# Decoding float64 weights in an attention and max-out kernel: a whole-word shift, a sign written by ScalarE, and a first-layer split in two instructions

## The chip, the cores and the metric

The kernel runs on one core of a Trainium2 chip. A core has a matrix engine (TensorE, PE in the profile, with its weight loads as PEld), VectorE (DVE), ScalarE (ACT), GpSimd (POOL) and a queue engine (SyncE, SP), which run their own instruction queues side by side and wait for each other by semaphores. The metric is the device time of one execution in microseconds; the time of a kernel is the median of its runs.

## The reference, cut to what matters

```python
# q, k, v: (8, 12, 448, 64)
q_n, k_n = rmsnorm(q, g_q), rmsnorm(k, g_k)      # over the last axis
scores = q_n @ k_n^T / sqrt(64)
attn = softmax(scores)
x = (attn @ v), heads side by side -> (3584, 768)
h = max(x @ w1, x @ w2, x @ w3)                  # w1, w2, w3: 768 x 768
out = (h @ w_out).astype(float32)                # w_out: 768 x 768
```

q, k, v and the gains come as float32. The four weight matrices come as float64, since they are scaled by a float64 number: each weight is two 32-bit words, and the kernel has to turn them into float32 and then into a pair of float16 parts.

## The kernel before, in words

**Attention.** The 96 heads are taken in pairs: 48 groups g, with the feed-forward part of a batch of six groups queued behind them. A group is 12 beats (`beat(g, i)`, i from 0 to 11), and for each of its four quarters c of the queries there are three beats. In the first, ScalarE makes the exponentials (`softmax`), TensorE multiplies the scores of the next quarter and, in the first six groups (g < PLAIN), transposes the exponentials of the quarter before (`turned`, two tiles per quarter); in the second, ScalarE copies those transpositions to SBUF (`pt`); in the third, VectorE takes the row maxima (`nm`) of the next scores. The first six groups work in float32 and turn their queries and keys on TensorE (`rows`, copied by ScalarE to `kt` and `qt`); the later groups work with pairs of float16 parts, and their weights are written as an upper part by ScalarE and a lower part by VectorE (`pp`). `thirds()` mixes the matmuls of the feed-forward part into the beats as it is queued.

**The order is written by hand.** Each engine runs its instructions in the order in which the program names them. `later(n, work)` puts a piece of work n beats on; work with `last=True` comes behind all other work of its beat. Nothing is reordered by a planner. Tiles of the PSUM pool `ps_m` (tag "m") have three buffers in turn, shared by `rows`, `turned`, `marks`, `most`, `spread` and `acc`: a new tile waits until the reader of the tile that had its buffer is done.

**Weights.** Blocks of 768 weights a partition are decoded one by one: 18 blocks of w1, w2, w3 at every fourth beat, then 6 blocks of w_out at every eighth (`BLOCK_BEATS`). A block is loaded into one of two `raw` buffers as pairs of words, low word first. In the profiled program `prep_block` does at its beat the rebias on ScalarE (the upper word, read as a float32, times 2^-112, in place), and two, three and four beats on the three stages of `decode` on VectorE: the top three bits of the low word are shifted down (from half-words), the sign is taken from the upper word into the low word's upper half, and one instruction shifts the upper word left by three and ORs the low word in. That gives the block as float32 in the place of its float16 parts. The next load into the buffer is issued one beat after the last stage (blocks of w_out: nine beats after the first).

**The first-layer split.** For every three blocks, `bound_in` measures a bound: 18 matmuls into `marks`, a maximum on VectorE (`most`, L172), a transposition (L157), a maximum over a row (`top`, L160), a matmul that spreads it (L164, again a tile named `most`), one VectorE instruction that reads it (L273), a root on GpSimd and three small instructions that make the scale `up`. Then each of the three blocks is split at steps of four beats: ScalarE scales it in place (L289) and casts it to float16 (L290), and two beats later GpSimd subtracts this from the scaled block (L293). The blocks of w_out are split in another way already: a scaled cast on ScalarE (L329) and one VectorE instruction (L334).

Of the kernel before, what the change touches and what calls it, by code (L numbers as in the profile page):

```python
# [8 lines left out]

F32 = mybir.dt.float32  # L10
U32 = mybir.dt.uint32
U16 = mybir.dt.uint16
BF16 = mybir.dt.bfloat16
F16 = mybir.dt.float16
AF = mybir.ActivationFunctionType
ALU = mybir.AluOpType
# [7 lines left out]
REBIAS = 2.0 ** -112  # L24
# [22 lines left out]
def qknorm_attention_maxout_ffn_kernel(  # L47
# [35 lines left out]
    nc = tc.nc  # L83
# [36 lines left out]
    def later(beats, work, last=False):  # L120

        due.setdefault(clock[0] + beats, ([], []))[last].append(work)
# [26 lines left out]
    def largest(column, done, gaps):  # L149


        top = sb.tile([1, 1], F32, name="top", bufs=2)
        box = []

        def turn():
            box.append(ps_m.tile([P, 512], F32, name="marks", tag="m"))
            nc.tensor.matmul(box[0][0:1, 0:P], column, ident, start=True, stop=True)  # L157

        def reduce():
            nc.vector.tensor_reduce(top, box[0][0:1, 0:P], axis=AX, op=ALU.max)  # L160

        def spread():
            box.append(ps_m.tile([P, 512], F32, name="most", tag="m"))
            nc.tensor.matmul(box[1][:, 0:1], ones, top, start=True, stop=True)  # L164

        at = 0
        for gap, work in zip(gaps, (turn, reduce, spread, lambda: done(box[1][:, 0:1]))):
            at += gap
            later(at, work)

    def row_largest(dst, src):
        nc.vector.tensor_reduce(dst, src, axis=AX, op=ALU.max, apply_absolute_value=True)  # L172
# [4 lines left out]
    w_sb = const.tile([P, NFT * NJ + 1, 2, NCT * P], F16, name="w_sb")  # L177
# [9 lines left out]
    def rebias(raw):  # L187


        upper = raw.bitcast(F32).rearrange("p (n t) -> p n t", t=2)[:, :, 1]  # L190
        nc.scalar.activation(upper, upper, AF.Copy, scale=REBIAS)

    def decode(raw, f, stage):

        words = raw.bitcast(U16).rearrange("p (n t) -> p n t", t=4)
        bits = raw.rearrange("p (n t) -> p n t", t=2)
        if stage == 0:
            nc.vector.tensor_scalar(
                out=words[:, :, 0], in0=words[:, :, 1], scalar1=13, scalar2=None,
                op0=ALU.logical_shift_right,  # L200
            )
        elif stage == 1:
            nc.vector.tensor_scalar(
                out=words[:, :, 1], in0=words[:, :, 3], scalar1=0x8000, scalar2=None,
                op0=ALU.bitwise_and,
            )
        else:
            nc.vector.scalar_tensor_tensor(
                out=f.bitcast(U32), in0=bits[:, :, 1], scalar=3, in1=bits[:, :, 0],
                op0=ALU.logical_shift_left, op1=ALU.bitwise_or,  # L210
            )
# [22 lines left out]
    def plain(t, n):  # L234
        return t[:, n + 1].rearrange("p a n -> p (a n)").bitcast(F32)

    def prep_block(n):
        kind, ft, j = blocks[n]
        raw = raws[n]
        f = plain(w_sb, n) if kind == "in" else plain(wo_sb, ft)  # L240
        rebias(raw)

        for stage in range(3):
            later(2 + stage, lambda stage=stage: decode(raw, f, stage), True)
        if kind == "out":
            later(5, lambda: row_largest(o_row[:, ft:ft + 1], f), True)
        later(5 if kind == "in" else 9, load_raw)
        if j == NJ - 1:
            later(5, lambda: bound_in(ft), True)
        elif kind == "out" and ft == NFT - 1:  # L250
            later(6, bound_out)

    def bound_in(ft):

        most = sb.tile([P, 1], F32, name="most", bufs=2)
        box = []

        def products():
            box.append(ps_m.tile([P, 512], F32, name="marks", tag="m"))
            for at in range(NJ * NCT):  # L260
                n, c = divmod(at, NCT)
                f = plain(w_sb, ft * NJ + n).bitcast(BF16)
                f = f.rearrange("p (n t) -> p n t", t=2)[:, c * P:(c + 1) * P, 1]
                nc.tensor.matmul(
                    box[0][:, 0:P], f, f, start=at == 0, stop=at == NJ * NCT - 1
                )

        def reduce():
            row_largest(most, box[0][:, 0:P])
            largest(most, clear, (2, 2, 3, 1))  # L270

        def clear(bound):
            nc.vector.tensor_scalar(  # L273
                out=most, in0=bound, scalar1=SQUARE, scalar2=LEAST ** 2,
                op0=ALU.mult, op1=ALU.max,
            )
            nc.gpsimd.tensor_tensor(out=w_up[:, ft:ft + 1], in0=most, in1=root, op=ALU.pow)
            later(2, scale)

        def scale():  # L280
            top, up = w_most[:, ft:ft + 1], w_up[:, ft:ft + 1]
            nc.vector.tensor_copy(top, up)
            nc.vector.reciprocal(up, top)
            nc.vector.tensor_scalar(
                out=up, in0=up, scalar1=2.0 * UP, scalar2=None, op0=ALU.mult
            )

            def upper(n, f):
                nc.scalar.activation(f, f, AF.Copy, scale=up)  # L289
                nc.scalar.copy(w_sb[:, n, 0], f)  # L290

            def lower(n, f):
                nc.gpsimd.tensor_tensor(  # L293
                    out=w_sb[:, n, 1], in0=f, in1=w_sb[:, n, 0], op=ALU.subtract
                )

            for j in range(NJ):
                n = ft * NJ + j
                f = plain(w_sb, n)
                later(2 + 4 * j, lambda n=n, f=f: upper(n, f), True)  # L300
                later(4 + 4 * j, lambda n=n, f=f: lower(n, f), True)

        later(2, products)
        later(4, reduce)
# [632 lines left out]
    for i, src in enumerate((g_q, g_k)):  # L937
        nc.scalar.dma_start(
            out=gains[:, i], in_=src.rearrange("(o d) -> o d", o=1).broadcast_to([P, D])
# [75 lines left out]
    def beat(g, i):  # L1015
# [102 lines left out]
        if decoded[0] < len(blocks) and clock[0] > due_at:  # L1118
            later(0, lambda n=decoded[0]: prep_block(n), True)
            decoded[0] += 1  # L1120
# [42 lines left out]
```

## Time and profile before

| What | Value |
|---|---|
| median of three runs | 1051.09 us (1048.96 to 1051.29) |
| the profiled execution | 1049.89 us, of which its span is 1047.7 us |
| TensorE, VectorE, ScalarE, GpSimd busy | 95%, 68%, 61%, 60% of the span |
| granted TensorE clock over the span | 0.99 |
| rebias (L191), first and last start | 19.5 and 217.4 us, 24 instructions |
| the split's cast (L290), first and last start | 68.5 and 190.4 us, 18 instructions |

The page counts for each engine how long its instructions ran; idle time is put down to what ended last before the engine went on. A group of instructions is a source line with its tiles: busy time, the mean of one, and the idle time just before them with its releaser. The timeline has the start and the duration of single instructions, with the idle time before them in brackets. Engines overlap, so busy time alone says nothing about the end; the work that a stage waits for does. The chain of waits that ended last is on TensorE from 430 us on.

### The profile page before, as it was taken

Reading aid. Unit: us, or ns where it says so; the run is one execution under the profiler, and the core shown is the slowest. Engines: PE = TensorE matmul, PEld = TensorE weight load, DVE = VectorE, ACT = ScalarE, POOL = GpSimd, SP = SyncE. Lnnn points to the kernel's source line nnn. Section 1 sums busy time; section 2 is a strip of 40 time slices with the busy share of each in tenths; the row PEclk is TensorE's granted clock in tenths of the full one; section 3 lists DMA queues with packets and bytes.
Section 4 is the critical chain, followed back from the end, with each engine's and each line's share of the span. In section 5 each row is a group of like instructions: output and inputs, shape, how many; then the busy total and the mean of one; then the engine's idle time right before and its main releaser. Section 6 shows DMA issues by size and latency. Waiting matters only on the chain.

```text
span 1047.7 us, 17338 instructions
## 1 busy us (share of the span) xinstructions
PE 991.5 (95%) x5958; PEld 530.3 (51%) x5958; DVE 707.5 (68%) x1322; ACT 638.6 (61%) x1437; POOL 625.9 (60%) x667
## 2 busy tenths in 40 slices
PE   4988879897899999999999999999999999999998
PEld 3554544343445555455555555555555555555555
DVE  4988889898667766677676857776677657661120
ACT  3778887666666576656666666666565776651101
POOL 5657899865766676666766666667567765500000
PEclk9999989999999999999999999999999999999999
DMA  7756579997898999998999999998999998762001
GB/s 170 192 156 168 138 171 209 186 168 130 181 180 168 170 180 205 159 178 171 201 174 185 159 197 191 168 184 167 201 175 177 173 195 149 134 103 71 1 1 61
DMA packets 524888, 166.19 MB, mean 159 GB/s; under 512 B 501120, under 2 KB 520576, under 8 KB 524800
## 3 DMA queue, kind: packets, MB, share of 16 engines
q1 hardware_dynamic: 461792, 149.09, 73.9%
q10 hardware_dynamic: 63008, 16.00, 8.6%
q8 instruction: 47, 0.77, 0.3%
q14 instruction: 41, 0.34, 0.1%
HBM read 53.54 MB, written 11.01 MB: 62 GB/s over the span
## 4 chain that ended last, share of the span: by engine, by line
PE 59%; DVE 0%; ACT 0%; issue 0%
PE acc L812 34%; PE acc L872 12%; PE av L783 6%; PE sc L603 6%; PE sc L610 1%; DVE pp L737 0%; DVE nm L625 0%; DVE ss L405 0%; ACT osb L881 0%; ACT qp L447 0%; PE most L534 0%; ACT ht L832 0%; DVE ht L836 0%
## 5 line engine op out<-in xcount | busy, mean ns | idle before, releaser
L812 PE MATMUL acc<-xt,w_sb 128*128 128x448 f16 x2592 | 516.2, 354 | 0.0
L812 PEld LDWEIGHTS <-w_sb 128*128 128x128 f16 x2592 | 252.2, 98 | 244.9 <-issue 15.8
L641 ACT ACTIVATE sc<-sc,nm 128x448 f32<-128x448 f32 x294 | 178.7, 608 | 188.9 <-DVE nm L625 184.3
L625 DVE TENSOR_REDUCE nm<-sc 128x2 f32<-128x896 f32 x192 | 186.1, 969 | 102.0 <-PE sc L610 51.1
L727 ACT ACTIVATE pp<-sc,rs 128x448 f16<-128x448 f32 x294 | 173.1, 634 | 81.0 <-ACT sc L641 27.9
L737 DVE SCALAR_TENSOR_TENSOR pp<-sc,rs,pp 128x448 f16<-128x448 f32 x294 | 188.0, 675 | 4.3 <-ACT pp L727 4.3
L419 POOL TENSOR_TENSOR ri<-ri,half_neg 128x7 f32<-128x7 f32 x96 | 146.7, 1529 | 8.0
L872 PE MATMUL acc<-wo_sb,ht 128*128 128x384 f16 x864 | 149.0, 328 | 0.0
L841 POOL COPY hx<-ht 128x128 f16<-128x128 f16 x48 | 16.1, 336 | 213.9 <-DVE ht L836 213.4
L603 PE MATMUL sc<-kt,qt 128*128 128x448 f16 x504 | 116.6, 354 | 12.8 <-DVE pp L737 8.4
L872 PEld LDWEIGHTS <-ht 128*128 128x128 f16 x864 | 84.0, 99 | 60.5 <-issue 6.1
L453 POOL TENSOR_TENSOR kp<-kn,kp 128x448 f16<-128x448 f32 x42 | 43.9, 1044 | 72.0 <-ACT kp L447 72.0
L603 PEld LDWEIGHTS <-qt 128*128 128x128 f16 x504 | 48.3, 98 | 59.3 <-DVE pp L737 11.4
L783 PE MATMUL av<-pt,vp 128*64 128x448 f16 x672 | 72.2, 356 | 0.1
L405 DVE TENSOR_REDUCE ss<-sq 128x7 f32<-128x448 f32 x96 | 57.6, 601 | 11.9 <-ACT sq L396 8.7
L720 DVE TENSOR_SCALAR rs<-sc 128x2 f32<-128x2 f32 (+1 forms) x168 | 26.3, 157 | 53.5 <-ACT sc L641 53.5
L798 DVE SCALAR_TENSOR_TENSOR xt<-av,xt 128x448 f16<-128x448 f32 x42 | 26.2, 623 | 51.9 <-ACT xt L797 51.9
L565 POOL TENSOR_TENSOR vp<-vr,vp 128x512 f16<-128x512 f32 x42 | 50.0, 1191 | 8.7 <-ACT vp L559 8.7
L826 DVE TENSOR_TENSOR m<-acc,m 128x448 f32<-128x448 f32 x48 | 29.6, 618 | 37.7 <-PE acc L812 37.5
L453 POOL TENSOR_TENSOR qp<-qn,qp 128x448 f16<-128x448 f32 x42 | 44.2, 1052 | 16.7 <-ACT qp L447 16.3
L783 PEld LDWEIGHTS <-vp 128*64 128x64 f16 x672 | 34.9, 109 | 34.4 <-issue 14.5
L832 ACT ACTIVATE ht<-acc 128x448 f16<-128x448 f32 x48 | 26.3, 547 | 41.7 <-DVE acc L826 41.7
(128 smaller groups left out, 1251.5 us busy)
## 6 DMA issues: line engine op xcount, KB each, us to landing
raw<-in_moe_w_dram SPq DMA_DIRECT2D x18, 768.0 KB, 4.5
kt<-kt SPq DMA_DIRECT2D x84, 112.0 KB, 2.3
vr<-in_v_dram SPq DMA_DIRECT2D x48, 192.0 KB, 4.0
out_dram<-osb SPq DMA_DIRECT2D x24, 384.0 KB, 3.4
kr<-in_k_dram ACTq DMA_DIRECT2D x34, 224.0 KB, 3.8
qr<-in_q_dram ACTq DMA_DIRECT2D x34, 224.0 KB, 4.4
raw<-in_moe_w_out_dram SPq DMA_DIRECT2D x6, 768.0 KB, 5.9
vs<-vp SPq DMA_DIRECT2D x84, 48.0 KB, 2.1
```

The source lines that it names most:

```text
L405: nc.vector.tensor_reduce(sums[g % 2][:, KQ[what]], sq, axis=AX, op=ALU.add)
L419: nc.gpsimd.tensor_tensor(out=ri, in0=ri, in1=half_neg[:, at], op=ALU.pow)
L453: nc.gpsimd.tensor_tensor(out=parts[:, :, 1], in0=n, in1=parts[:, :, 0], op=ALU.subtract)
L565: nc.gpsimd.tensor_tensor(out=vp[:, 1], in0=values_of(g).rearrange("p h n d -> p (h n) d"), in1=vp[:, 0], op=ALU.subtract,)
L603: nc.tensor.matmul(sc[:, h, :S], qt[:, 4 * h + c], kt[:, n, keys[h]], start=n == 0, stop=n == 1,)
L625: nc.vector.tensor_reduce(nm[:, :n], sc[:, :n, :S], axis=AX, op=ALU.max, negate=True)
L641: nc.scalar.activation(to, sc[:, h, :S], AF.Exp, bias=nm[:, h:h + 1], accum_out=total,)
L727: nc.scalar.activation(pp[:, h, 0], sc[:, h, :S], AF.Copy, scale=rs[:, h:h + 1])
L737: nc.vector.scalar_tensor_tensor(out=pp[:, h, 1], in0=sc[:, h, :S], scalar=rs[:, h:h + 1], in1=pp[:, h, 0], op0=ALU.mult, op1=ALU.subtract,)
L783: nc.tensor.matmul(av[half, :S], values, pt[:, 7 * h + block, SHIFT[h]:SHIFT[h] + S], start=n == 0, stop=n == len(steps) - 1,)
L812: nc.tensor.matmul(acc[:, :S], wt[:, wp, c], xs[c][:, xp], start=(c == 0 and n == 0), stop=(c == NCT - 1 and n == 2),)
L872: nc.tensor.matmul(acc[:, :HW], lhs, wo_sb[:, f, wp, half * HW:(half + 1) * HW], start=(f == 0 and n == 0), stop=(f == NFT - 1 and n == 2),)
```

## The change

The low word's three bits are shifted as one 32-bit word by 29 (this clears its upper half). The sign is no longer taken by VectorE: ScalarE writes the upper word times 2^-112 as a float16 into the low word's upper half, where it is a zero with the weight's sign, and then does the rebias as before. The order of the stages turns round: the shift comes at the block's own beat, sign and rebias two beats on, the OR at the fourth beat as before. In the first-layer split, ScalarE scales and casts in one instruction, and VectorE in place of GpSimd takes the lower part from the unscaled block in one instruction.

```diff
         upper = raw.bitcast(F32).rearrange("p (n t) -> p n t", t=2)[:, :, 1]
+        sign = raw.bitcast(F16).rearrange("p (n t) -> p n t", t=4)[:, :, 1]
+        nc.scalar.activation(sign, upper, AF.Copy, scale=REBIAS)
         nc.scalar.activation(upper, upper, AF.Copy, scale=REBIAS)
 
     def decode(raw, f, stage):
 
-        words = raw.bitcast(U16).rearrange("p (n t) -> p n t", t=4)
         bits = raw.rearrange("p (n t) -> p n t", t=2)
         if stage == 0:
             nc.vector.tensor_scalar(
-                out=words[:, :, 0], in0=words[:, :, 1], scalar1=13, scalar2=None,
+                out=bits[:, :, 0], in0=bits[:, :, 0], scalar1=29, scalar2=None,
                 op0=ALU.logical_shift_right,
             )
         elif stage == 1:
-            nc.vector.tensor_scalar(
-                out=words[:, :, 1], in0=words[:, :, 3], scalar1=0x8000, scalar2=None,
-                op0=ALU.bitwise_and,
-            )
+            rebias(raw)
...
-        rebias(raw)
-
-        for stage in range(3):
-            later(2 + stage, lambda stage=stage: decode(raw, f, stage), True)
+        decode(raw, f, 0)
+        later(2, lambda: decode(raw, f, 1), True)
+        later(4, lambda: decode(raw, f, 2), True)
...
             def upper(n, f):
-                nc.scalar.activation(f, f, AF.Copy, scale=up)
-                nc.scalar.copy(w_sb[:, n, 0], f)
+                nc.scalar.activation(w_sb[:, n, 0], f, AF.Copy, scale=up)
 
             def lower(n, f):
-                nc.gpsimd.tensor_tensor(
-                    out=w_sb[:, n, 1], in0=f, in1=w_sb[:, n, 0], op=ALU.subtract
+                nc.vector.scalar_tensor_tensor(
+                    out=w_sb[:, n, 1], in0=f, scalar=up, in1=w_sb[:, n, 0],
+                    op0=ALU.mult, op1=ALU.subtract,
                 )
```

Line numbers of the new kernel are some lines lower behind the changed places. The places in each engine's order that the text speaks of follow. They are of a group in the part where blocks are decoded and split while the first six groups run.

VectorE, from the maximum of a group's last quarter to the first of the next one, before:

```order
L625 TENSOR_REDUCE nm<-sc 128x1
L791 TENSOR_TENSOR av<-av,by 128x448
L203 TENSOR_SCALAR raw<-raw 128x768
L208 SCALAR_TENSOR_TENSOR w_sb<-raw 128x768
L160 TENSOR_REDUCE top<-marks 1x1
L798 SCALAR_TENSOR_TENSOR xt<-av,v_up,xt 128x448
L625 TENSOR_REDUCE nm<-sc 128x2
```

and of the change:

```order
L621 TENSOR_REDUCE nm<-sc 128x1
L787 TENSOR_TENSOR av<-av,by 128x448
L288 SCALAR_TENSOR_TENSOR w_sb<-w_sb,w_up 128x768
L205 SCALAR_TENSOR_TENSOR w_sb<-raw 128x768
L198 TENSOR_SCALAR raw<-raw 128x768
L159 TENSOR_REDUCE top<-marks 1x1
L794 SCALAR_TENSOR_TENSOR xt<-av,v_up,xt 128x448
L621 TENSOR_REDUCE nm<-sc 128x2
```

Ahead of `top`, the sign (L203) has gone, and the lower half (L288) and the shift of the next block (L198) have come.

ScalarE, between the copy of a sum (`by`) and the first exponentials of the next group, before:

```order
L289 ACTIVATE w_sb<-w_sb,w_up 128x768
L290 CAST w_sb<-w_sb 128x768
L674 COPY pt<-turned 128x4x128 x2
L641 ACTIVATE e,sum<-sc,nm 128x448
L797 ACTIVATE xt<-av,v_up 128x448
L191 ACTIVATE raw<-raw 128x768
L674 COPY pt<-turned 128x4x128 x2
L289 ACTIVATE w_sb<-w_sb,w_up 128x768
L290 CAST w_sb<-w_sb 128x768
L641 ACTIVATE e,sum<-sc,nm 128x448 x2
```

and of the change:

```order
L285 ACTIVATE w_sb<-w_sb,w_up 128x768
L670 COPY pt<-turned 128x4x128 x2
L191 ACTIVATE raw<-raw 128x768
L192 ACTIVATE raw<-raw 128x768
L637 ACTIVATE e,sum<-sc,nm 128x448
L793 ACTIVATE xt<-av,v_up 128x448
L670 COPY pt<-turned 128x4x128 x2
L285 ACTIVATE w_sb<-w_sb,w_up 128x768
L191 ACTIVATE raw<-raw 128x768
L192 ACTIVATE raw<-raw 128x768
L637 ACTIVATE e,sum<-sc,nm 128x448 x2
```

Two casts and a rebias have gone; a pair of sign (L191) and rebias (L192) stands ahead of each of the two exponentials.

TensorE, over the same beats, with the engines' semaphores that an instruction waits for in brackets; before, from the transposition of the third quarter's second tile on:

```order
L662 MATMUL turned<-ident,e 128x128 [waits DVE_49]
L662 MATMUL turned<-ident,e 128x128 x2
L664 MATMUL turned<-ident,e 128x128
L664 MATMUL turned<-ident,e 64x128
L594 MATMUL sc<-kt,qt 128x448 [waits Activation_49]
L594 MATMUL sc<-kt,qt 128x448
L662 MATMUL turned<-ident,e 128x128 [waits PE_49]
L662 MATMUL turned<-ident,e 128x128 x2
L664 MATMUL turned<-ident,e 128x128
L664 MATMUL turned<-ident,e 64x128
L482 MATMUL rows<-ident,kn 128x128 [waits Activation_49,Pool_49]
```

and of the change:

```order
L658 MATMUL turned<-ident,e 128x128 [waits Activation_49]
L658 MATMUL turned<-ident,e 128x128 x2
L660 MATMUL turned<-ident,e 128x128
L660 MATMUL turned<-ident,e 64x128
L590 MATMUL sc<-kt,qt 128x448 [waits Activation_49]
L590 MATMUL sc<-kt,qt 128x448
L658 MATMUL turned<-ident,e 128x128 [waits Activation_49]
L658 MATMUL turned<-ident,e 128x128 x2
L660 MATMUL turned<-ident,e 128x128
L660 MATMUL turned<-ident,e 64x128
L478 MATMUL rows<-ident,kn 128x128 [waits DVE_49,Pool_49]
```

The buffers of `ps_m` fall to other tiles: the wait for VectorE (for `top`, whose tile had the buffer) has gone from the first row to the last one. In the same way the transposition behind the next scores, which waited for L273, now waits for ScalarE's copy to `kt`, and the turned queries behind the values' matmuls wait for L273 (L269 in the new kernel).

1 line of the change is left out of this document (removed).

## The prediction, before the run

> **What bounds the kernel now.** I read four views: busy time by stretch, TensorE's waits by stretch, the groups of instructions, and the timeline of one group of heads. The first, with idle TensorE as length less busy:
>
> ```profile
> core 0: us, PE busy (x) PEld busy (x) DVE busy (x) ACT busy (x) POOL busy (x), PEclk, DMA share, GB/s
> 20.00:62.00 42.00, 37.58 (x231) 23.59 (x233) 38.44 (x50) 28.47 (x66) 24.66 (x24) 1.00 0.73 187
> 62.00:140.00 78.00, 63.94 (x439) 38.12 (x435) 66.49 (x87) 65.00 (x133) 62.49 (x47) 0.98 0.57 153
> 140.00:200.00 60.00, 50.81 (x284) 25.08 (x284) 53.94 (x95) 44.20 (x90) 53.27 (x46) 0.93 0.91 182
> 200.00:340.00 140.00, 128.69 (x743) 65.46 (x743) 107.35 (x206) 90.45 (x204) 91.97 (x99) 0.97 0.92 169
> 340.00:1047.70 707.70, 702.60 (x4239) 373.10 (x4235) 433.80 (x863) 403.68 (x933) 385.07 (x441) 1.00 0.84 153
> ```
>
> From 340 us on TensorE idles 5.1 us in 708: there its work is the time. Between 20 and 340 us it idles 4.4 + 14.1 + 9.2 + 11.3 = 39.0 us. The weights are decoded and split only in the early part (the source rows below), so nothing but those 39 us can be won, while what TensorE loses there is lost in full, since its work behind is the same. VectorE is busy for 86 to 92% of each stretch up to 200 us and ScalarE and GpSimd come close behind: every queue is nearly full, so the order in a queue matters more than the sum. TensorE's waits: one of 20 to 62 us, three of 62 to 140, one of 140 to 200 and one of 200 to 340:
>
> ```profile
> PE most L534 <- DVE v_most L527: 1.0, 1, 1.0
> PE turned L662 <- DVE top L160: 4.1, 3, 1.4
> PE sc L594 <- ACT e L641: 3.7, 3, 2.2
> PE turned L662 <- DVE most L273: 2.7, 2, 1.4
> PE sc L610 <- DVE pp L737: 4.7, 3, 3.0
> PE sc L603 <- DVE pp L737: 6.0, 3, 2.7
> ```
>
> In the first six groups of heads (up to about 140 us) the waits are for two tiny VectorE instructions queued behind the decoding, and for ScalarE's exponentials; later for VectorE's pp.
>
> **The change part by part.** The groups it touches, with two nearest rows for what is new (L329, L334):
>
> ```profile
> L198 DVE TENSOR_SCALAR raw<-raw 128x768 uint16<-128x768 uint16 x24 | 28.4, 1182 | 0.0
> L203 DVE TENSOR_SCALAR raw<-raw 128x768 uint16<-128x768 uint16 x24 | 29.3, 1222 | 0.8
> L293 POOL TENSOR_TENSOR w_sb<-w_sb 128x768 f16<-128x768 f32 x18 | 32.6, 1810 | 8.9 <-ACT w_sb L290 8.9
> L290 ACT CAST w_sb<-w_sb 128x768 f16<-128x768 f32 x18 | 15.0, 832 | 3.4 <-POOL w_sb L293 2.2
> L191 ACT ACTIVATE raw<-raw 128x768 f32<-128x768 f32 x24 | 22.6, 942 | 5.2 <-DMA raw<-in_moe_w_dram 5.2
> L720 DVE TENSOR_SCALAR rs<-sc 128x2 f32<-128x2 f32 (+1 forms) x168 | 26.3, 157 | 53.5 <-ACT sc L641 53.5
> L334 DVE SCALAR_TENSOR_TENSOR wo_sb<-wo_sb,o_block 128x768 f16<-128x768 f32 x6 | 7.2, 1197 | 2.9 <-ACT wo_sb L329 2.9
> L329 ACT ACTIVATE wo_sb<-wo_sb,o_block 128x768 f16<-128x768 f32 x6 | 5.6, 937 | 2.4 <-DVE wo_sb L334 2.2
> L198 DVE TENSOR_SCALAR raw<-raw x24: 1011/1034/1759, 23.3 to 220.0; 128x768 uint16<-128x768 uint16 x24
> L208 DVE SCALAR_TENSOR_TENSOR w_sb<-raw x18: 939/959/2168, 28.6 to 140.3; 128x768 uint32<-128x768 uint32 x18
> L191 ACT ACTIVATE raw<-raw x24: 882/920/1417, 19.5 to 217.4; 128x768 f32<-128x768 f32 x24
> ```
>
> VectorE loses 24 sign instructions (-29.3 us) and gains 18 lower halves at L334's 1.20 us (+21.5 us, same operands and shapes). ScalarE loses 18 casts (-15.0 us), its scaled cast is L329's instruction (0.94 us, as L289 before), and it gains 24 sign writes. These are bounded by a contiguous half-word write (L290, 0.83 us) and L191's slowest (1.42); I take L191's median 0.92, same stride: +22.1 us. GpSimd loses 32.6 us.
>
> The whole-word shift is not in the trace. From above: the half-word shift's mean, 1.18 us. [...] I take 1.03, the half-word shift's median, since instruction, count and stride are equal: no gain. [...]
>
> The sums say little; the places say more. One group of heads:
>
> ```profile
> 89.85 0.83 ACT L290 CAST w_sb<-w_sb 128x768 f16<-128x768 f32 x1
> 90.59 1.06 ACT L674 COPY pt<-turned 128x512 f32<-128x512 f32 x2
> 91.28 2.17 DVE L208 SCALAR_TENSOR_TENSOR w_sb<-raw 128x768 uint32<-128x768 uint32 x1
> 92.69 0.92 ACT L191 ACTIVATE raw<-raw 128x768 f32<-128x768 f32 x1
> 93.37 0.27 DVE L160 TENSOR_REDUCE top<-marks 1x1 f32<-1x128 f32 x1
> 93.51 0.56 ACT L674 COPY pt<-turned 128x512 f32<-128x512 f32 x1
> 93.70 0.55 PE L662 MATMUL turned<-ident,e 128*128 128x128 f32 x3 [1.38 <-DVE top L160]
> 94.50 0.59 ACT L674 COPY pt<-turned 128x512 f32<-128x512 f32 x1 [0.42 <-PE turned L664]
> 94.98 0.94 ACT L289 ACTIVATE w_sb<-w_sb,w_up 128x768 f32<-128x768 f32 x1
> 96.01 0.83 ACT L290 CAST w_sb<-w_sb 128x768 f16<-128x768 f32 x1
> 96.75 0.63 ACT L641 ACTIVATE e<-sc,nm 128x448 f32<-128x448 f32 x1
> 98.14 1.02 PE L594 MATMUL sc<-kt,qt 64*128 64x448 f32 x4 [0.74 <-ACT e L641]
> 101.21 0.55 PE L662 MATMUL turned<-ident,e 128*128 128x128 f32 x3 [1.36 <-DVE most L273]
> ```
>
> *Buffers.* In the new order the transposition that waited for top (93.70) waits for a ScalarE copy already made, and top is owed only to the turned rows two steps later; the one that waited for most (101.21) waits for kt, and most is owed behind the values' matmuls. Both waits, 1.38 and 1.36 us, go even though VectorE's path to top grows: it is now the lower half (1.20), the combine and a shift, where it was the sign and the combine.
>
> *ScalarE.* Between the copies at 90.59 and the exponential at 96.75 there now stand two pairs of rebias and sign in place of one rebias. The copies can start where the cast did, 89.85: 0.74 us earlier. Gone are the rebias (0.82, 92.69 to 93.51) and half a microsecond of the wait for the stalled transposition (93.51 to 94.50 is 0.99, where a copy takes half of 1.06). The split's part shrinks from 1.77 (94.98 to 96.75) to 0.85, taken as one of L329's less the 0.1 by which neighbours overlap. Added are two pairs at 0.82 + 1.00 each; the second of a pair waits for the first, as the cast at 96.01 starts 1.03 behind its source. So -0.74 - 0.82 - 0.50 - 0.92 + 3.64 = +0.66 us: the exponential comes that much later, and the scores at 98.14 with it. The first stall is thus eaten by ScalarE; the second (1.36) is a gain. Per group 0.66 - 1.36 = -0.7.
>
> Two groups have the whole pattern (-1.4); the third of the three waits for top has no wait for most behind it, so that group pays +0.7: for 62 to 140 us **-0.7 us**. For 20 to 62 us, where no split runs yet, VectorE loses a sign with each block and ScalarE gains one: **0**, bounds -1.0 (all of a wait for VectorE's v_most) and +2.1. The +2.1 is the longest wait for a weight load: the shift, not the rebias, now meets the load first, on VectorE, and the score maxima queue behind it, and the exponentials behind those. L191's row has 5.2 us of such waits in all; the signs removed, 1.22 us per block, cover them.
>
> From 140 us on the timeline names these:
>
> ```profile
> 140.56 0.35 PE L534 MATMUL most<-v_most,ones_c 128*128 128x1 f32 x2 [3.28 <-ACT qp L447]
> 147.21 2.29 DVE L203 TENSOR_SCALAR raw<-raw 128x768 uint16<-128x768 uint16 x1
> 152.99 0.57 PE L610 MATMUL sc<-kt,qt 128*64 128x448 f16 x4 [3.01 <-DVE pp L737]
> 215.69 0.93 PE L603 MATMUL sc<-kt,qt 128*128 128x448 f16 x4 [1.46 <-DVE pp L737]
> ```
>
> The v_most matmul waits for exponentials that get two pairs ahead of them: +1.6. The pp wait 12 us later loses the 2.29 us sign, gets a lower half of 1.2 and starts 1.6 later, inside its 3.0 us of slack: the two cancel. Over the rest of the stretch blocks of w_out come at half the pace of the splits, so VectorE gets two lower halves for each sign it loses, 2 x 1.20 - 1.22 = +1.2 us, three or four times; it idles 6.1 us there, and GpSimd, busy for 53 of 60 us, loses 1.81 us with each split. [...] I take **-0.5**. Past 200 us the splits are over and the last signs (shifts run to 220.0) go from in front of the pp waits: **-0.7**, half of the stall at 215.69.
>
> Sum: -0.7 + 0 + 0 - 0.5 - 0.7 = **-1.9 us**. The profiled execution took 1049.89 us around its span of 1047.7, and 1048.0 would follow; the median of the runs is 1051.09, 1.2 above it, so I forecast **1049.2**. About 0.3%, 3.2 us, is what a measurement of this kernel can tell from none.
>
> **Rivals.** *The shift halves* (0.25): at 0.55 us VectorE is relieved by some 0.5 to 0.6 us per block more. [...] It would also take half the pp waits from 140 us to the stall at 215.69 (4.7 + 1.5, so -3.1) and half of the 3.3 us at 140.56: -1.9 - 3.1 - 1.6 = -6.6, 1044.5. [...]
>
> *ScalarE's pair becomes the stall* (0.17), the slower side. Place: the two pairs ahead of the exponentials at 96.75. If a sign lasts L191's 1.42, each pair costs 0.5 more and the exponential comes 1.7 us late (0.66 + 1.0); it decides once that passes the 1.36 us given back, and then all six plain groups pay about 1.1: +6.6, less the later gains of 1.2: +5.4, 1056.5. For it: ScalarE works 65 of 78 us there; against: 13 of them are idle.
>
> *Loads wait on VectorE* (0.08): the 5.2 us of load waits reach TensorE in full: -1.9 + 5.2 = +3.3, 1054.4. Against: VectorE's shift stands at the same step as the rebias did, and ScalarE, freed of the wait, makes up part of it.
>
> **How the numbers follow.** Forecast 0.50, with its own range 1046 to 1052.5: faster 0.11, same 0.35, slower 0.04 of it. The halved shift: 0.23 faster, 0.02 same. The pair: 0.03 same, 0.14 slower. Loads: 0.05 same, 0.03 slower. Together 0.34, 0.45, 0.21. The range from 1043.5 to 1055 takes in the first rival, and of the second its smaller half.
>
> **What would show it.** In the new profile: the shift near 1.03 (0.55: first rival); signs at 0.9; the waits for top and most gone; scores waiting for e in the first groups some 0.7 us longer; TensorE idle for some 13.4 us of that stage. Wrong would be: idle time of TensorE past 340 us changed, or maxima waiting for raw.

## The result: slower by 1.8%

| | before | changed |
|---|---|---|
| median of the runs, us | 1051.19 (1048.96 to 1052.34) | 1070.22 (1068.28 to 1070.38) |
| ratio, 95% interval | | 1.0179 (1.0159 to 1.0200) |
| span of the profiled execution, us | 1047.7 | 1068.7 |
| TensorE busy, us | 991.5 | 998.9 |
| TensorE idle in the span, us | 56.2 | 69.8 |
| mean granted clock of TensorE | 0.990 | 0.979 |

The change costs 19 us where a gain of about 2 was forecast, and the time lies outside the range. The span grew by 21.0 us: 13.6 us are idle time of TensorE, and 7.4 us are the same 5958 matmuls running longer. One of the twelve executions of a run below, with the sign back on VectorE (1168.01 us, granted clock 0.848), was in the chip's slower state; it is in that run's median but not in its ratio, and gains and losses between runs are taken from ratios.

The groups of instructions of the changed kernel that are new or moved (the columns as before: busy us and mean ns of one, then the idle time ahead and what ended it):

```profile
L191 ACT ACTIVATE raw<-raw 128x768 f16<-128x768 f32 x24 | 46.5, 1936 | 0.0
L192 ACT ACTIVATE raw<-raw 128x768 f32<-128x768 f32 x24 | 21.5, 896 | 0.8
L198 DVE TENSOR_SCALAR raw<-raw 128x768 uint32<-128x768 uint32 x24 | 16.9, 704 | 1.6 <-DMA raw<-in_moe_w_dram 1.6
L205 DVE SCALAR_TENSOR_TENSOR w_sb<-raw 128x768 uint32<-128x768 uint32 x18 | 17.3, 958 | 25.0 <-ACT raw L192 25.0
L285 ACT ACTIVATE w_sb<-w_sb,w_up 128x768 f16<-128x768 f32 x18 | 17.1, 949 | 0.0
L288 DVE SCALAR_TENSOR_TENSOR w_sb<-w_sb,w_up 128x768 f16<-128x768 f32 x18 | 19.6, 1090 | 0.2 <-ACT w_sb L285 0.2
L198 DVE TENSOR_SCALAR raw<-raw x24: 548/556/1397, 17.7 to 235.2; 128x768 uint32<-128x768 uint32 x24
```

Two prices are far from the ones taken. The sign write (L191, the row with float16 out) lasts 1.94 us, not 0.92, and not within the bounds of 0.83 to 1.42. The whole-word shift has a median of 0.556 us, not 1.03: that is the first rival's price. The scaled cast (0.95) is as forecast (0.94), and the lower half (1.09) a little shorter than forecast (1.20). New as well is the fourth row: VectorE sits idle ahead of its combine for 25.0 us in all, because the word that it combines is still being rebiased. The exponentials wait little for VectorE in this kernel (1.8 us for its maxima from 20 to 62 us, and no such wait stands in the list for 62 to 140 us), so this idle time is not what holds up the scores.

Busy time by stretch:

```profile
20.00:62.00 42.00, 32.53 (x205) 21.43 (x205) 25.43 (x35) 35.13 (x63) 18.34 (x19) 1.00 0.65 164
62.00:140.00 78.00, 62.39 (x388) 36.73 (x390) 48.76 (x84) 68.21 (x120) 33.59 (x35) 0.91 0.54 139
140.00:200.00 60.00, 48.35 (x278) 25.23 (x279) 44.35 (x84) 45.91 (x83) 33.97 (x33) 0.86 0.76 161
200.00:340.00 140.00, 125.38 (x706) 62.71 (x704) 105.56 (x202) 95.61 (x205) 88.81 (x94) 0.95 0.90 167
```

TensorE's longest waits from 20 to 62, 62 to 140 and 140 to 200 us (us in total, times, longest):

```profile
PE sc L590 <- ACT e L637: 7.9, 4, 2.4
PE sc L590 <- ACT e L637: 18.0, 7, 4.7
PE most L163 <- ACT m L818: 4.2, 1, 4.2
```

and of the kernel before, from 20 to 62 us:

```profile
PE sc L594 <- ACT e L641: 1.2, 3, 0.7
```

From 20 to 140 us the scores wait 25.9 us for ScalarE's exponentials, against 4.9 before; the waits for `top` and `most`, 6.8 us before, have left the list for 62 to 140 us, as forecast. VectorE is no longer the fullest engine there (48.8 of 78 us against 66.5); ScalarE is (68.2). Between 20 and 340 us TensorE idles 51.3 us, against 39.0.

The matmuls that bound a finished set of three blocks come once per group of heads and so show the pace. First and last of the six, of the kernel before and then of the changed one:

```profile
44.69 1.21 PE L264 MATMUL marks<-w_sb 128*128 128x128 bf16 x18
145.91 1.21 PE L264 MATMUL marks<-w_sb 128*128 128x128 bf16 x18
```

```profile
47.10 1.19 PE L260 MATMUL marks<-w_sb 128*128 128x128 bf16 x18 [0.75 <-ACT pt L670]
162.67 1.21 PE L260 MATMUL marks<-w_sb 128*128 128x128 bf16 x18
```

Five groups took 101.2 us before and take 115.6 us now: 20.2 and 23.1 us each. The loss is no single accident but 2.9 us per group on the average, about 1 us for each of its three blocks; by the sixth group 16.8 us are lost.

Part of one such group, some of ScalarE's and TensorE's rows from the timeline of the changed kernel:

```profile
103.27 1.02 PE L590 MATMUL sc<-kt,qt 64*128 64x448 f32 x4 [1.52 <-ACT e L637]
103.64 1.07 ACT L670 COPY pt<-turned 128x512 f32<-128x512 f32 x2
...
104.58 0.96 ACT L285 ACTIVATE w_sb<-w_sb,w_up 128x768 f16<-128x768 f32 x1
105.42 1.92 ACT L191 ACTIVATE raw<-raw 128x768 f16<-128x768 f32 x1
107.37 0.88 ACT L192 ACTIVATE raw<-raw 128x768 f32<-128x768 f32 x1
108.15 0.62 ACT L637 ACTIVATE e<-sc,nm 128x448 f32<-128x448 f32 x1
...
109.53 1.78 PE L590 MATMUL sc<-kt,qt 64*128 64x448 f32 x4 [3.20 <-ACT e L637]
```

and the view by windows of 6 us around it, with the first half of the second window by itself in the third row (the last three numbers are the granted clock, the DMA share and GB/s):

```profile
104.00:110.00 6.00, 2.80 (x20) 2.26 (x20) 4.49 (x8) 5.97 (x13) 0.00 (x0) 0.97 0.80 208
110.00:116.00 6.00, 6.00 (x28) 2.84 (x26) 5.26 (x11) 5.97 (x12) 4.30 (x6) 0.74 0.42 134
110.00:113.00 3.00, 3.00 (x12) 1.72 (x9) 2.26 (x8) 3.00 (x9) 1.55 (x3) 0.50 0.81 259
116.00:122.00 6.00, 6.00 (x53) 3.99 (x50) 3.38 (x5) 3.17 (x8) 4.90 (x4) 1.00 0.41 131
```

ScalarE has no gap between the copy at 103.64 and the exponential at 108.15: split, sign and rebias stand back to back in front of it, and the scores wait 3.20 us. The four score matmuls that follow take 1.78 us where the same four took 1.02 us six microseconds earlier. The windows show a slower clock behind the wait: in the 6 us with the wait TensorE was busy for 2.80, and in the next 3 us its granted clock is 0.50 (0.74 over 6 us). The same is seen a group earlier: TensorE was busy for 0.80 us from 82 to 86 us, and its clock from 86 to 90 us is 0.60. So these two waits, 3.20 us each, were paid twice, first as idle time and then as a slower clock.

### The profile page after: what moved, and what is told of

Its sections match the earlier page's. It is cut to its first block, busy times and chain, and to the rows that moved or that the text cites. A ratio compares the mean times of both kernels' runs of the same rounds, so it can differ in the third digit from the quotient of the medians.

```text
span 1068.7 us, 17306 instructions
## 1 busy us (share of the span) xinstructions
PE 998.9 (93%) x5958; PEld 534.1 (50%) x5958; DVE 679.6 (64%) x1316; ACT 667.8 (62%) x1443; POOL 580.4 (54%) x649
## 4 chain that ended last, share of the span: by engine, by line
PE 56%; DVE 1%; ACT 0%; DMA 0%; POOL 0%; SPq 0%; issue 0%
PE acc L808 32%; PE acc L868 12%; PE av L779 6%; PE sc L599 6%; PE sc L606 1%; DMA vs<-vp 0%; DVE nm L621 0%; POOL ri L415 0%; ACT sc L637 0%; DVE ss L401 0%; SPq L572 0%; DVE pp L733 0%; ACT osb L877 0%; ACT qp L443 0%; PE most L530 0%
## 5 line engine op out<-in xcount | busy, mean ns | idle before, releaser
L599 PEld LDWEIGHTS <-qt 128*128 128x128 f16 x504 | 48.5, 99 | 60.5 <-DVE pp L733 13.6
L401 DVE TENSOR_REDUCE ss<-sq 128x7 f32<-128x448 f32 x96 | 57.7, 602 | 11.7 <-ACT sq L392 8.3
L716 DVE TENSOR_SCALAR rs<-sc 128x2 f32<-128x2 f32 (+1 forms) x168 | 26.3, 157 | 58.9 <-ACT sc L637 58.9
L590 PE MATMUL sc<-kt,qt 64*128 64x448 f32 (+1 forms) x96 | 30.1, 702 | 24.4 <-ACT e L637 23.5
```

The source lines that it names most:

```text
L401: nc.vector.tensor_reduce(sums[g % 2][:, KQ[what]], sq, axis=AX, op=ALU.add)
L599: nc.tensor.matmul(sc[:, h, :S], qt[:, 4 * h + c], kt[:, n, keys[h]], start=n == 0, stop=n == 1,)
```

## The experiments

### Part by part

**ScalarE's sign write with the new order.** The kernel before with the sign written by ScalarE, in the new order, which comes with it; half-word shift and the old split stay:

```diff
+        nc.scalar.activation(sign, upper, AF.Copy, scale=REBIAS)
         nc.scalar.activation(upper, upper, AF.Copy, scale=REBIAS)
...
         elif stage == 1:
-            nc.vector.tensor_scalar(
-                out=words[:, :, 1], in0=words[:, :, 3], scalar1=0x8000, scalar2=None,
-                op0=ALU.bitwise_and,
-            )
+            rebias(raw)
...
-        rebias(raw)
-
-        for stage in range(3):
-            later(2 + stage, lambda stage=stage: decode(raw, f, stage), True)
+        decode(raw, f, 0)
+        later(2, lambda: decode(raw, f, 1), True)
+        later(4, lambda: decode(raw, f, 2), True)
```

> The kernel before with one part of the change alone: ScalarE writes the sign as a float16 zero ahead of the rebias, and the pair stands two beats behind the shift, as in the change; shift on half words and split as before. Theory A (the sign write of 1.93 us stands ahead of ScalarE's exponentials, TensorE waits for these, and the longer gaps lower its granted clock): the loss is all here, about +20 us or more over the kernel before (1068 to 1078), TensorE's waits for e in the stretch from 62 to 140 us at 15 us or more against 3.7, granted clock there at 0.93 or less. Theory B (the lower half's move to VectorE is the cause): within 4 us of the kernel before. Theory C (the new order, in which the shift and not the rebias meets the load first, is the cause): also slow, but then the third run beside this, which keeps the order and puts the sign back, is slow too.

Measured: 1083.21 us, ratio 1.0303 (1.0272 to 1.0335). TensorE's waits for e from 62 to 140 us are 15.7 us and its clock there is 0.85. Theory A's marks for the waits and the clock are met, and the time lies beyond its range (1068 to 1078): sign write and order together lose some 32 us by the ratio, more than the whole change.

**The split alone.** Kernel before with

```diff
-                nc.scalar.activation(f, f, AF.Copy, scale=up)
-                nc.scalar.copy(w_sb[:, n, 0], f)
+                nc.scalar.activation(w_sb[:, n, 0], f, AF.Copy, scale=up)
...
-                nc.gpsimd.tensor_tensor(
-                    out=w_sb[:, n, 1], in0=f, in1=w_sb[:, n, 0], op=ALU.subtract
+                nc.vector.scalar_tensor_tensor(
+                    out=w_sb[:, n, 1], in0=f, scalar=up, in1=w_sb[:, n, 0],
+                    op0=ALU.mult, op1=ALU.subtract,
```

> The kernel before with the split alone changed: upper half by one scaled cast of ScalarE, lower half by one VectorE instruction with the scale folded in; shift, sign and rebias as before. Theory A: no loss, since ScalarE is relieved of 0.83 us per split while VectorE gains 1.0 us per split: within 4 us of the kernel before, 1047 to 1055. Theory B: most of the loss, 1065 or more.

Measured: 1050.53 us, ratio 0.9999 (0.9982 to 1.0016). Theory B is out. ScalarE is busy for 14.5 us less (624.1 against 638.6) and VectorE for 10.2 us more (717.7 against 707.5). These 10 us are fewer than what the 18 lower halves take (21.6 us in the run with shift and split below), and the combine is shorter where GpSimd no longer subtracts: a mean of 0.99 us for the blocks of the first layer in that run, against 1.27 with the shift alone.

**The shift alone.** Kernel before with

```diff
-                out=words[:, :, 0], in0=words[:, :, 1], scalar1=13, scalar2=None,
+                out=bits[:, :, 0], in0=bits[:, :, 0], scalar1=29, scalar2=None,
```

> The kernel before with the whole-word shift alone (one word read and written in place of one half word). The trace of the changed kernel has it at 0.556 us in place of 1.03 (median) or 1.18 (mean). If VectorE's queue sets the waits between 62 and 340 us, as the prediction's first rival had it, 24 shifts that are 0.5 to 0.6 us shorter give 3 to 5 us: 1046 to 1048. If these waits are set elsewhere, no change within 2 us.

Measured: 1044.11 us, ratio 0.9936 (0.9916 to 0.9957): 6.7 us gained by the ratio, somewhat more than the 3 to 5 expected.

**The changed kernel with the sign back on VectorE**, everything else as changed:

```diff
-        nc.scalar.activation(sign, upper, AF.Copy, scale=REBIAS)
...
+        elif stage == 3:
+            words = raw.bitcast(U16).rearrange("p (n t) -> p n t", t=4)
+            nc.vector.tensor_scalar(
+                out=words[:, :, 1], in0=words[:, :, 3], scalar1=0x8000, scalar2=None,
+                op0=ALU.bitwise_and,
+            )
...
+        later(3, lambda: decode(raw, f, 3), True)
```

> The changed kernel with the sign write alone put back on VectorE (half words, at the beat between the rebias and the combine); whole-word shift, split and the order (shift first, rebias two beats later) stay changed. Theory A: the loss goes, and what the relieved VectorE is worth shows: 1043 to 1050, granted clock between 62 and 200 us back to 0.97 or more. Theory B and C: still slow, 1064 to 1072.

Measured: 1052.24 us, ratio 1.0010 (0.9996 to 1.0025). The large loss goes with the sign, as theory A had it, and theory C, the order as the main cause, is out. But theory A's range is missed: the gain of the shift isn't there, and the clock from 62 to 200 us did not come back to 0.97 (0.93 and 0.89). Something else in the change eats some 8 us; the order was left as a suspect.

### What the layouts cost

The kernel before with more instructions behind its work, each kind three times, all with 768 elements per partition (fs, fd: every other float32 word of two buffers; hd, hs: one half word in four; hd2: one in two; hd1, flat: contiguous; hs lies in the source's own buffer; u4, u2, u1 and w2, w1 are the same layouts for VectorE's half words and words, with s for the source and d for the destination). ScalarE's seven that are shown stand at L1151 to L1161 and L1165, two lines apart; VectorE's shifts are u4d from u4s at L1167, u2d from u2s at L1169, u1d from u1s at L1171, u1d from u4s at L1173, u4d from u1s at L1175, w2d from w2s at L1177 and w1d from w1s at L1179:

```diff
+        nc.scalar.activation(fd, fs, AF.Copy, scale=REBIAS)
+        nc.scalar.activation(hd, fs, AF.Copy, scale=REBIAS)
+        nc.scalar.activation(hs, fs, AF.Copy, scale=REBIAS)
+        nc.scalar.activation(hd2, fs, AF.Copy, scale=REBIAS)
+        nc.scalar.activation(hd1, fs, AF.Copy, scale=REBIAS)
+        nc.scalar.activation(hd, flat, AF.Copy, scale=REBIAS)
...
+        nc.scalar.activation(hd, fs, AF.Copy, scale=1.0)
+        nc.vector.tensor_scalar(out=u4d, in0=u4s, scalar1=1, scalar2=None, op0=ALU.logical_shift_right)
...
```

> The kernel before with 51 more instructions behind its work, on idle engines and on two free buffers, each kind three times with 768 elements per partition: ScalarE's scaled copy in eight layouts (float32 in every other word to float32 in every other word; to one half word in four, in another buffer and in place; to one half word in two; to a contiguous row; from contiguous words to one half word in four and to a contiguous row; one half word in four with scale 1, so that no value underflows) and VectorE's shift in nine (one half word in four, in two, contiguous, scattered source alone, scattered destination alone, and the same for whole words). Theory 1 (a half word written with gaps costs twice a word on either engine): ScalarE 1.93 us wherever half words are written with gaps and about 0.9 elsewhere, the scale and the buffer make no difference; VectorE 1.0 wherever half words are written with gaps. Theory 2 (the value: results that underflow are slow): 1.93 for all float16 results but the one with scale 1, which takes 0.9. Theory 3 (in place, two views of one word): 1.93 in place alone.

The groups by line, of one execution:

```profile
L1151 ACT ACTIVATE raw<-raw 128x768 f32<-128x768 f32 x3 | 2.6, 875 | 4.8 <-DVE raw L1135 4.7
L1153 ACT ACTIVATE raw<-raw 128x768 f16<-128x768 f32 x3 | 5.7, 1895 | 0.1
L1155 ACT ACTIVATE raw<-raw 128x768 f16<-128x768 f32 x3 | 5.7, 1916 | 0.1
L1157 ACT ACTIVATE raw<-raw 128x768 f16<-128x768 f32 x3 | 3.2, 1073 | 0.1
L1159 ACT ACTIVATE raw<-raw 128x768 f16<-128x768 f32 x3 | 2.6, 881 | 0.1
L1161 ACT ACTIVATE raw<-raw 128x768 f16<-128x768 f32 x3 | 5.7, 1904 | 0.1
L1165 ACT ACTIVATE raw<-raw 128x768 f16<-128x768 f32 x3 | 5.7, 1900 | 0.1
L1169 DVE TENSOR_SCALAR raw<-raw 128x768 uint16<-128x768 uint16 x3 | 1.8, 594 | 0.1
L1171 DVE TENSOR_SCALAR raw<-raw 128x768 uint16<-128x768 uint16 x3 | 1.1, 360 | 0.1
L1173 DVE TENSOR_SCALAR raw<-raw 128x768 uint16<-128x768 uint16 x3 | 1.7, 560 | 0.1
L1175 DVE TENSOR_SCALAR raw<-raw 128x768 uint16<-128x768 uint16 x3 | 3.1, 1019 | 0.1
L1177 DVE TENSOR_SCALAR raw<-raw 128x768 uint32<-128x768 uint32 x3 | 1.7, 561 | 0.1
L1179 DVE TENSOR_SCALAR raw<-raw 128x768 uint32<-128x768 uint32 x3 | 1.7, 560 | 0.1
```

On ScalarE a float16 result costs 1.90 us when it goes to one half word in four, and 0.88 when it goes to a contiguous row (L1159). The source's layout doesn't matter (L1161), nor does the buffer (L1155), nor a scale that lets nothing underflow (L1165): theories 2 and 3 are out. VectorE has the same penalty: 1.02 us with the scattered destination alone (L1175), 0.56 with the scattered source alone (L1173). Whole words at the same distance of eight bytes cost nothing extra (on ScalarE L1151 beside the contiguous half words of L1159, on VectorE L1177 beside L1179). Theory 1 holds with one correction: one half word in two (L1157, L1169) costs only 1.07 and 0.59. So it isn't the gap as such but half words that are written eight bytes apart; why four bytes are mild these runs don't tell.

### Price or place

**The same pair, the write made short.** The sign goes as a contiguous row into the place that the combine fills later, so this kernel leaves the signs of the weights out:

```diff
-    def rebias(raw):
+    def rebias(raw, f):
...
-        sign = raw.bitcast(F16).rearrange("p (n t) -> p n t", t=4)[:, :, 1]
+        sign = f.bitcast(F16)[:, 0:DM]
```

> The changed kernel, but the sign is written as a contiguous row of float16 (into the place that the combine fills two beats later) instead of into one half word in four: the same instruction at the same place, 0.88 us by the run with the layouts instead of 1.93. Left out by this: the signs don't reach the weights. Theory A1 (only the price of the write was wrong; ScalarE has some 13 us to spare in the early part and the change is slow because 24 x 1.93 less 18 x 0.83 = 31 us were added, here 24 x 0.88 - 15 = +6): no loss, 1042 to 1050, TensorE's waits for e from 62 to 140 us under 6 us, granted clock between 62 and 200 us 0.95 or more. Theory A2 (any pair ahead of the exponentials is too much, whatever its length): still 5 us or more above the kernel before, 1056 to 1062.

Measured: 1053.86 us, ratio 1.0027 (1.0001 to 1.0052). Its row:

```profile
L191 ACT ACTIVATE w_sb<-raw 128x768 f16<-128x768 f32 x18 | 16.3, 907 | 0.0
```

With the write at 0.91 us instead of 1.94 the ratio falls by 0.0152, 16 of the 19 us. That is the price, and A2 is out. But A1's range is missed by 4 us too, the waits for e from 62 to 140 us are still 9.7 us, and the clock is 0.88 and 0.86 from 62 to 140 and 140 to 200 us: as with the sign back on VectorE, the shift's gain is missing. TensorE's time shows what the long write costs and what it doesn't: here TensorE is busy for 999.1 us of a span of 1055.1, so it idles 56.0 us, as before the change (56.2), and works 7.6 us longer. The changed kernel has nearly the same work (998.9) and 13.8 us more idle time. So the write's length is paid in idle time; the slower clock is there without it. The busy times on the page of the run with the short write:

```profile
PE 999.1 (95%) x5958; PEld 534.9 (51%) x5958; DVE 680.3 (64%) x1316; ACT 644.1 (61%) x1443; POOL 581.3 (55%) x649
```

**Every second block's sign back on VectorE:**

```diff
+        half = n % 2
...
+        if not half:
+            nc.scalar.activation(sign, upper, AF.Copy, scale=REBIAS)
...
+        if half:
+            later(3, lambda: decode(raw, f, 3, half), True)
```

> The changed kernel with every second block's sign put back on VectorE, so that 12 sign writes of 1.93 us are left on ScalarE. Budget theory (loss = what ScalarE gains beyond its spare 13 us: 33 us lost at +46, 19 at +31): 12 x 1.93 - 15 = +8 us, no loss: 1044 to 1052. Local theory (each block whose pair stands ahead of an exponential delays that group on its own): half the loss, 1058 to 1063.

Measured: 1060.92 us, ratio 1.0104 (1.0083 to 1.0126). That is half way between no sign on ScalarE (1.0010) and all of them (1.0179). My budget theory, a spare of 13 us that has to be used up before anything is lost, falls; the local one stands: each long write delays its own group.

### The order

**Whole-word shift and split in the old order** (rebias with the load, shift two beats later, sign on VectorE): the edits of the run with the shift alone and of the run with the split alone, together.

> The kernel before with the whole-word shift and the split, in the old order (rebias with the load, shift two beats later, sign on VectorE). The shift alone gave 1044.1 us, the split alone 1050.5, and both together in the new order with the sign on VectorE 1052.2. If the new order (shift first, rebias two beats later) is what took the shift's gain away there, this runs at 1042 to 1047. If the lower half on VectorE uses up the time that the shift frees, it runs at 1049 to 1053.

Measured: 1043.72 us, ratio 0.9937 (0.9914 to 0.9961). The shift's gain is whole. So it was the new order that took it with the sign back on VectorE: 1.0010 less 0.9937 is 0.0073, about 8 us. Waits from 20 to 62 us, of VectorE and ScalarE; the new order (sign back on VectorE) first, the old order (this run) below:

```profile
DVE raw L205 <- ACT raw L191: 4.4, 3, 1.8
ACT e L643 <- DVE nm L627: 7.9, 5, 2.1
```

```profile
DVE raw L203 <- ACT raw L191: 0.4, 1, 0.4
ACT e L641 <- DVE nm L625: 0.6, 3, 0.2
```

With the rebias two beats later, VectorE's sign instruction stands waiting for it (4.4 us against 0.4), the maxima queue behind that, and ScalarE's exponentials wait for the maxima (7.9 us against 0.6). VectorE's wait runs back to ScalarE. In the profiled executions TensorE idles 3.5 us more for it (54.7 against 51.2 us), and its matmuls take 3.0 us more (996.9 against 993.9).

**One of the two moves at a time**, on the kernel just shown; shift early, and rebias late:

```diff
         rebias(raw)
+        decode(raw, f, 0)
-        for stage in range(3):
+        for stage in (1, 2):
```

> The kernel with whole-word shift and split in the old order (1043.7 us), with the shift alone moved two beats forward, to the beat of the load, where it stood in the changed kernel; rebias with the load on ScalarE, sign on VectorE. With shift and rebias both moved it took 1052.2. Theory V (VectorE now meets the load first, maxima and v_most queue behind it): 1049 to 1053. Theory S (the rebias two beats later, ahead of ScalarE's exponentials, is the cost): 1042 to 1046.

```diff
-        rebias(raw)
+        later(2, lambda: rebias(raw), True)
```

> The kernel with whole-word shift and split in the old order (1043.7 us), with the rebias alone moved two beats back, where it stood in the changed kernel; the shift two beats behind the load as before, sign on VectorE. Theory S (the rebias two beats later stands ahead of ScalarE's exponentials, and sign and combine on VectorE wait for it or go later): 1049 to 1053. Theory V (the shift's early place on VectorE is the cost): 1042 to 1046.

Measured: 1046.15 us, ratio 0.9958 (0.9942 to 0.9973), and 1047.32 us, ratio 0.9968 (0.9952 to 0.9984). Neither theory: each move seems to cost a part, 0.0021 and 0.0031 over 0.9937, and the intervals of the three overlap. Only both together stand clear of the old order. From 20 to 140 us the exponentials' waits for maxima come to 1.8 us in the old order, 6.7 with the shift early, 12.0 with the rebias late and 15.6 with both: they rank as the times do.

**The pair parted.** The changed kernel with the rebias back at the load; the long sign write stays where it was:

```diff
+        rebias(raw)
         decode(raw, f, 0)
...
-            rebias(raw)
+            nc.scalar.activation(sign, upper, AF.Copy, scale=1.0)
```

> The changed kernel with the rebias put back to the beat of the load; only the sign write (from the rebiased word, same layout, 1.9 us) stays two beats later on ScalarE, so that the pair is parted. By the sum of the runs so far the changed kernel's 19 us are 16 to 18 for the length of the write and 8.5 for the new order, less 6 to 7 for the shift. Theory S with A1 (length and the late rebias each cost on their own): the 8.5 go, 1060 to 1064. If the length of the write alone sets it: 1067 to 1071. If only the pair as one block of 2.8 us ahead of an exponential hurts: 1050 or less.

Measured: 1062.65 us, ratio 1.0116 (1.0097 to 1.0136), in the range of the first reading. Taking the rebias back to the load is worth 0.0063, some 7 us, and the long write keeps the kernel slow. This move parts the pair and ends the late rebias at once; which of the two counts, the run does not tell.

### A version that beats both

**The sign as a whole word too**, by one VectorE instruction, on the kernel with shift and split in the old order:

```diff
-            nc.vector.tensor_scalar(
-                out=words[:, :, 1], in0=words[:, :, 3], scalar1=0x8000, scalar2=None,
-                op0=ALU.bitwise_and,
-            )
+            nc.vector.scalar_tensor_tensor(
+                out=bits[:, :, 0], in0=bits[:, :, 1], scalar=0x80000000, in1=bits[:, :, 0],
+                op0=ALU.bitwise_and, op1=ALU.bitwise_or,
+            )
```

> The kernel with whole-word shift and split in the old order (1043.7 us), with the sign written by VectorE as a whole word too: one instruction takes the top bit of the upper word and joins it to the shifted lower word, in place of the half-word AND. No half word is written with gaps any more. It has the operands of the combine, which took 0.94 to 0.96 us undisturbed where the half-word AND takes 1.01 to 1.04, and like the combine it may be held up by GpSimd. Expected: 0.08 us per block, 2 us of VectorE's time in all, so 1042 to 1046, no difference from 1043.7 that can be told; if the second source collides with GpSimd as the combine's did (up to 2.17), 1046 to 1052.

Measured: 1043.52 us, ratio 0.9935 (0.9919 to 0.9952). Like the shift alone and shift with split it is 0.6% faster than the kernel before; the three can't be told apart. The new instruction has a median of 0.95 us, as expected, and a mean of 1.12 (the longest 1.77). That it is the second source which meets GpSimd's work no run shows.

## Why the prediction was wrong

**The step that failed: the sign write's price.** "These are bounded by a contiguous half-word write (L290, 0.83 us) and L191's slowest (1.42); I take L191's median 0.92, same stride: +22.1 us." It lasts 1.94, so the 24 writes took 46.5 us. By the prediction's own sum, two signs that are 1.02 us longer make +0.66 us per group some +2.7 (an estimate from these rows); 2.9 us per group were lost, which hold the effects of the order and of the clock as well. One row had half words, the other the stride, and neither had both; a bound needs the nearest row with the same combination. That row stood in the fence: VectorE's half-word shift, scattered in the same way, took 1.03 us, nearly twice what the whole-word shift turned out to take. The whole words at the same stride, 0.56 us, show that the half word is what costs.

**The whole-word shift** went wrong from the same cause, on the other side. I took 1.03; 0.556 was the first rival's price, and alone it gains 6.7 us where the rival's terms beyond the forecast gave 4.7. No row of the kernel before shows that rival's 0.55; what the runs showed is 0.556 in the changed kernel, 0.56 for whole words both eight bytes apart and contiguous (L1177, L1179), and 1.02 for half words written eight bytes apart (L1175).

**ScalarE's pair as the stall** was the rival with the right place and mechanism, the scores behind the exponentials behind the pair, at 1.42 a write and 1056.5. It measured 1.94 a write, and half the writes gave half the loss, so the mechanism scales. I held against it that 13 of 78 us of ScalarE were idle. The run with every second sign shows that this spare time doesn't help: it lies elsewhere in the group (ScalarE is busy for 3.17 us of 6 from 116 to 122 us, and for 5.97 in each of the two windows before).

**The order at +0.66 us per group** missed VectorE's side. I reckoned the later rebias as ScalarE's time only, not that VectorE's next decoding step waits for it with the maxima behind it. With the sign off ScalarE, the new order costs about 8 us that stand nowhere in the sum; the waits behind the -1.36 per group did go from the list, but no gain came of it, since the scores' waits for e grew. Had the write cost 0.91, the kernel would have run at 1053.9, inside the range, but by luck: the missed order and the missed shift nearly cancel.

**Past 340 us** the idle time was to stay: 5.1 us before, 6.3 now, which holds. What doesn't hold is "its work behind is the same": TensorE's work in the whole span grew by 7.4 us, at a granted clock of 0.979 in place of 0.990. No term of the sum had that. The two waits of 3.20 us are followed by a slower clock in the trace (0.60 and 0.50), but over the kernel the slower work does not grow with the idle time: with the short write it is 7.6 us at no more idle time than before. Which waits make it stays open.

**From 140 us on** the sum had -1.2 us; TensorE's idle time there, up to 340 us, grew from 20.5 to 26.3 us. No run shows its -0.5 us for 140 to 200 us: TensorE's idle time of that stretch grew from 9.2 to 11.7 us. The sixth of the plain groups now reaches to 162.67 us and the last shift to 235.2, and the runs don't separate what this lateness makes of it from what the decoding and the lower halves cost there. "Every queue is nearly full" was also too much: from 20 to 62 us ScalarE was busy for 68% and GpSimd for 59%.

**Loads on VectorE** didn't matter: the shift waited once, 1.6 us. **The split** alone changes nothing in the time.

How these parts add up: by ratios, the shift gives -0.0064, the split 0, the order +0.0073, the sign's move at the price of a short write +0.0017 (1.0027 less 1.0010, not to be told from nothing), its length +0.0152. The sum is +0.0178 against 0.0179 measured, but it had to come out: each part is the difference of two neighbours in one chain of runs that ends at the changed kernel. It divides the loss along that chain, with some 0.003 of uncertainty each, and doesn't show that nothing is missing; by another path the parts differ. Sign write and order on the kernel before, with the cast's 15 us still on ScalarE and the long shift, lost 0.0303, where the chain has 0.0242 for order, move and length. Which of these two made the rest was not tried.

## What to carry to other kernels

When an instruction isn't in the trace, take its price from a row with the same element size and the same stride together: two rows that each share one of them are no bounds. Half words written eight bytes apart cost about twice here what whole words eight bytes apart cost, on both engines (for 768 of them ScalarE 1.90 us against 0.88, VectorE 1.02 against 0.56), so bits are better moved as whole words where the layout lets them. And when a step moves to another beat, list who waits for it on the other engines: here, from 20 to 62 us, VectorE's sign waited 4.4 us for the later rebias in place of 0.4, and ScalarE's exponentials 7.9 us for the maxima queued behind it in place of 0.6.

## What the runs showed of the hardware that was not expected

- 768 half words written eight bytes apart: ScalarE 1.90 us against 0.88 contiguous, VectorE 1.02 against 0.36; with only the reads that far apart 0.56. Four bytes apart: 1.07 and 0.59. Whole words eight bytes apart: 0.88 and 0.56, on VectorE the same as contiguous words.
- TensorE's work after a long wait was longer: after 3.20 us of waiting, the granted clock was 0.50 for 3 us, and four score matmuls took 1.78 us instead of 1.02. Slower work makes up 7.4 of the 21.0 us lost, but it is as much (7.6) in the run with the short write, where TensorE idles no more than before; no run holds the clock.
- VectorE's combine of two sources had a mean of 1.35 us in the kernel before and 1.27 with the shift alone, but 0.99 with shift and split, where GpSimd no longer subtracts. In the kernel before, combines that ran while GpSimd subtracted took 2.16 and 2.17 us (at 76.05 and 91.28 us), and one that met no subtraction took 0.94 (at 107.08).
